# A routing search in six digits with wider steps, other spacings of its products, and one instruction pinned in order

## The chip, the cores and the metric

The kernel runs on one core of one Trainium2 chip. The metric is the device time of one execution in microseconds (us); for the kernel before it is the median of three runs. A profile is one more execution, recorded by the hardware profiler.

## The reference

Three layers follow one another: a gated linear attention, a dense layer with a leaky ReLU, and a mixture of eight experts. Only the last one's routing is touched:

```python
logits = x @ w_gate                       # 3072 tokens, 8 experts
order = np.argsort(-logits.flatten())
for idx in order:                         # best (token, expert) pair first
    tok, e = idx // E, idx % E
    if assigned[tok] >= 0 or counts[e] >= cap:   # cap = 3072 / 8 = 384
        continue
    assigned[tok] = e; counts[e] += 1
for e in range(E):                        # then each expert on its 384 tokens
    out[assigned == e] = np.maximum(x[assigned == e] @ w1[e], 0) @ w2[e]
```

The greedy pass is one long sequence: an expert that is full is closed, and its tokens go to their next choice.

## The kernel before

Attention and the first layer (`first`, `second`) take the span up to some 486 us. From there the main stream of TensorE is `layer2`: `second` for the last nine blocks of 128 tokens (products that write `xp`), the turning of the first expert's tokens (`xT`), and eight times `expert` (products that write `hp`, then `yp`). Each of these large products has 384 columns.

The routing (`route`) runs beside that stream, on VectorE with small products on TensorE. It makes seven rounds; each finds the expert that fills up first and the key of the last token that it takes, closes it, and hands a token list to `token_list` and a row of weight addresses to `fetch_weights`. In a round a 32-bit key is searched digit by digit (`LEVELS`: shift, bits, thresholds T). One level of the search is this chain: VectorE compares every token's value with T thresholds (`ge`); TensorE counts with `ge` as the weights (`c`, one product for each of NT/G = 24/(128/T) groups, of E*G columns); VectorE takes the diagonal (`cm`, `cd`); TensorE sums over partitions (`cnt`); VectorE compares with the room left (`ok`); TensorE joins the experts' bits (`tot`); VectorE finds the digit (`scr`) and takes it off the values (`v`), and the next level's `ge` follows. So T = 32 means six products of 32 columns, T = 16 three of 64 columns, and T = 64 twelve of 16 columns.

What sets the order of the instructions on each engine has two parts. A `Driver` writes the program: it adds up 160 ns for each large product (384 / 2.4) and lets a side stream go on when its pause has passed. The pauses of the routing are `GAP`: after the first comparison of a round (`GAP[4]`, 3400), after the comparison of the other levels (`GAP[0]`, 1700), after `cd` (`GAP[1]`, 700), after `ok` (`GAP[2]`, 550) and before a round's `ps` (`GAP[3]`, 2000). Then the planner of the tile framework orders each engine's instructions: of those that its own model of the times holds ready, it takes the one that the program has first. So a product whose inputs the model holds late goes further back, and a VectorE instruction that it holds ready early can move ahead of others. `keep_in_program_order` takes that freedom from one instruction: it is placed behind everything that the program already has on that engine.

At a round's end the program runs through `take`, `asg`, `un` into the next round (`m`, `eq0`, `key`, `am`, `v`, `oh`, `ge`, `dg`) with no pause until `GAP[4]`. The list of the finished round starts up to 300 ns of the driver's clock later, with `si`, `lo`, `hi`, `lob`, `hib`, and goes on with `ohs`, `h12`, `rh`, the products `pi` and `pj`, and the addresses `idx`, `row`.

`route_constants` prepares thresholds (`thr`, and scaled copies `thl`), selection and diagonal masks on VectorE just before the routing begins.

The profile gives all instructions one line, L84, since a helper records them; they are told apart by what they write.

Of the kernel before, what the change touches and what calls it, by code (L numbers as in the profile page):

```python
# [11 lines left out]
BF16 = mybir.dt.bfloat16  # L12
# [3 lines left out]
OP = mybir.AluOpType  # L16
# [75 lines left out]
def body(tc, qk, v, f_logit, w_in, w_out, w_gate, w1, w2, out):  # L92
    nc = tc.nc
    w_in, w_out = w_in.bitcast(I32), w_out.bitcast(I32)
    PE, DVE, ACT, POOL, SP = (InOrder(tc, e) for e in (nc.tensor, nc.vector, nc.scalar, nc.gpsimd, nc.sync))
# [6 lines left out]
    NT = B * S // 128  # L102
# [10 lines left out]
    with ExitStack() as ctx:  # L113
# [504 lines left out]

        LEVELS = [(27, 5, 32), (22, 5, 32), (17, 5, 32), (12, 5, 32), (7, 5, 32), (3, 4, 16), (0, 3, 16)]
        STEP = [2.0 ** (-6 * l) for l in range(len(LEVELS))]
        R = {}

        def route_constants():
            def const(name, shape, dt=F32):
                R[name] = rc.tile(shape, dt, name=name)
                return R[name]

            DVE.tensor_scalar(const("tri", [128, 128], BF16), column_less_row(rc, "jp"), 0.0, None, op0=OP.is_gt)  # L630
            DVE.memset(const("ones", [128, 128], BF16), 1.0)
            i128 = const("i128", [128, 128])
            POOL.iota(i128, pattern=[[1, 128]], base=0, channel_multiplier=0,
                      allow_small_or_imprecise_dtypes=True)
            const("place", [128, 384], F16)
            POOL.iota(const("i384", [128, 384]), pattern=[[1, 384]], base=1, channel_multiplier=0,
                      allow_small_or_imprecise_dtypes=True)
            DVE.tensor_scalar(const("i1", [128, 32]), i128[:, :32], 1.0, None, op0=OP.add)
            pi = const("pi", [128, 1], I32)
            DVE.tensor_copy(pi, pcol)  # L640
            for w in (4, 5):
                T, G = 2 ** w, 128 >> w
                thr = const(f"thr{w}", [128, NT // G, T, G], BF16)
                for a in range(NT // G):
                    DVE.tensor_copy(thr[:, a], R["i1"][:, :T, None].to_broadcast([128, T, G]))
                t = const(f"t{w}", [128, 1], I32)
                tf = const(f"tf{w}", [128, 1])
                DVE.tensor_scalar(t, pi, 7 - w, None, op0=OP.logical_shift_right)
                DVE.tensor_copy(tf, t)
                DVE.tensor_scalar(const(f"sel{w}", [128, T], F16), i128[:, :T], tf, None, op0=OP.is_equal)  # L650
                DVE.tensor_scalar(t, pi, G - 1, None, op0=OP.bitwise_and)
                DVE.tensor_copy(tf, t)
                d1 = const(f"d1{w}", [128, G])
                DVE.tensor_scalar(d1, i128[:, :G], tf, None, op0=OP.is_equal)
                DVE.tensor_copy(const(f"diag{w}", [128, E, G]), d1[:, None, :].to_broadcast([128, E, G]))
            m5 = rc.tile([128, 128], I32, name="m5")
            DVE.tensor_copy(m5, i128)
            DVE.tensor_scalar(m5, m5, 31, None, op0=OP.bitwise_and)
            m5f = rc.tile([128, 128], F32, name="m5f")
            DVE.tensor_copy(m5f, m5)  # L660
            DVE.tensor_scalar(t, pi, 2, None, op0=OP.arith_shift_right)
            sf = const("sf", [128, 1])
            DVE.tensor_copy(sf, t)
            DVE.tensor_scalar(const("join", [128, 128], F16), m5f, sf, None, op0=OP.is_equal)
            DVE.tensor_scalar(t, pi, 5, None, op0=OP.arith_shift_right)
            qf = const("qf", [128, 1])
            DVE.tensor_copy(qf, t)
            DVE.tensor_scalar(const("quarter", [128, 4]), i128[:, :4], qf, None, op0=OP.is_equal)
            DVE.tensor_copy(const("i12", [128, 12, NT], BF16), i128[:, :12, None].to_broadcast([128, 12, NT]))
            DVE.tensor_copy(const("jn", [128, 12, NT], BF16), i128[:, None, :NT].to_broadcast([128, 12, NT]))  # L670
            wd = const("wd", [128, E])
            DVE.tensor_scalar(wd, i128[:, :E], -1.0, float(E), op0=OP.mult, op1=OP.add)
            DVE.tensor_copy(const("wdt", [128, NT, E], BF16), wd[:, None, :].to_broadcast([128, NT, E]))
            DVE.tensor_copy(const("wdx", [128, E, NT], BF16), wd[:, :, None].to_broadcast([128, E, NT]))
            DVE.tensor_scalar(const("wdc", [128, 1]), pcol, -1.0, float(E), op0=OP.mult, op1=OP.add)

            pw = const("pw", [128, 1], I32)
            DVE.tensor_scalar(pw, R["wdc"], 127.0, None, op0=OP.add)
            DVE.tensor_scalar(pw, pw, 23, None, op0=OP.logical_shift_left)
            DVE.memset(const("bits", [128, 128], BF16), 0.0)  # L680
            DVE.tensor_scalar(R["bits"][:E], R["ones"][:E, :], pw.bitcast(F32)[:E], None, op0=OP.mult)
            for i in range(2):
                DVE.memset(const(f"cd{i}", [128, 128], F16), 0.0)
            DVE.tensor_scalar(const("p1024", [128, 1]), pcol, float(E * 128), None, op0=OP.add)

            n = len(LEVELS) - 1
            sh, mk = (const(x, [128, n, NT], I32) for x in ("sh", "mk"))
            unit = const("unit", [128, n, NT])
            for l, (s, w, T) in enumerate(LEVELS[1:]):
                POOL.memset(sh[:, l, :], s)  # L690
                POOL.memset(mk[:, l, :], 2 ** w - 1)
                POOL.memset(unit[:, l, :], STEP[l + 1])
            R["thr"] = [R["thr5"]]
            for l, (s, w, T) in enumerate(LEVELS):
                if l > 0:
                    t = R["thr5" if T == 32 else "thr4"]
                    u = rc.tile(list(t.shape), BF16, name=f"thl{l}")
                    DVE.tensor_scalar(u, t, STEP[l], None, op0=OP.mult)
                    R["thr"].append(u)
            DVE.tensor_scalar(const("i1s", [128, 16]), R["i1"][:, :16], STEP[-1], None, op0=OP.mult)  # L700

            DVE.tensor_copy(const("opn", [128, E]), wd)
            DVE.memset(const("un", [128, NT]), 1.0)
            DVE.memset(const("asg", [128, NT]), 0.0)
            DVE.memset(const("kcap", [128, 1]), float(NT * 128 // E))
            DVE.memset(const("smx", [128, 1]), 0.0)

        def small(shape, name, dt=F32, bufs=2):
            return rw.tile(shape, dt, name=name, bufs=bufs)

        def bank(shape, name):
            return banks[0].tile(shape, F32, name=name, tag="rt", bufs=RT)
# [3 lines left out]
        def route():  # L716
# [4 lines left out]
            wdx, kcap, un, asg, smx, ones, i1, opn = (R[x] for x in ("wdx", "kcap", "un", "asg", "smx", "ones", "i1", "opn"))  # L721
            last = [small([128, 1], f"last{i}", bufs=1) for i in range(2)]
            for rnd in range(E - 1):
# [17 lines left out]
                DVE.scalar_tensor_tensor(v, d0, 1.0, un, op0=OP.add, op1=OP.mult)  # L741
                for l, (sh, w, T) in enumerate(LEVELS):
                    G = 128 // T
                    ge = small([128, NT * 32], "ge", BF16)[:, :NT * T].rearrange("p (a t g) -> p a t g", t=T, g=G)
                    va = v.rearrange("p (a g) -> p a g", g=G)[:, :, None, :].to_broadcast([128, NT // G, T, G])
                    DVE.tensor_tensor(ge, va, R["thr"][l], op=OP.is_ge)
                    if l == 0:
# [13 lines left out]
                    with nc.allow_low_precision("one count and zeros"):  # L761
                        DVE.tensor_reduce(cd[:, :E], cm, axis=AX.X, op=OP.add)
                    yield GAP[1]
                    cnt = bank([128, 32], "cnt")
                    mm(cnt[:, :T], cd, R[f"sel{wt}"], True, True)
                    ok = small([128, 32], "ok", BF16)
                    DVE.tensor_scalar(ok[:, :T], cnt[:, :T], kcap, None, op0=OP.is_ge)
                    yield GAP[2]
                    tot = bank([128, 32], "tot")
                    mm(tot[:, :T], R["bits"], ok[:, :T], True, True)  # L770
                    J = small([128, 1], "J")
                    scr = small([128, 32], "scr")
                    DVE.tensor_scalar(scr[:, :T], tot[:, :T], STEP[l], None, op0=OP.min, op1=OP.add, accum_out=J)
                    if l + 1 < len(LEVELS):
                        vp = v
# [12 lines left out]
                                         op0=OP.is_equal, op1=OP.mult, accum_out=cg)  # L788
# [55 lines left out]
            DVE.tensor_scalar(wi, mx, -128.0, R["p1024"], op0=OP.mult, op1=OP.add)  # L844
            LISTS["w", r] = wi

        GAP = (1700.0, 700.0, 550.0, 2000.0, 3400.0)
        lists = []

        def slots_of(x, n):  # L850
# [17 lines left out]
        def token_list(r, s):  # L868

            si = small([128, NT], "si", I32)  # L870
            DVE.tensor_scalar(si, s, -1.0, None, op0=OP.add)
            lo = small([128, NT], "lo", I32)
            DVE.tensor_scalar(lo, si, 31, None, op0=OP.bitwise_and)
            hi = small([128, NT], "hi", I32)
# [7 lines left out]
            G = 4  # L882
# [447 lines left out]
```

## Time and profile before

| | |
|---|---|
| three runs | 784.7, 785.66, 787.34 us (median 785.66) |
| the profiled execution | 781.42 us, its span 779.6 us |
| TensorE's granted clock, mean | 0.983 |
| busy in the span | TensorE 730.7 us (94%), weight load 484.1, VectorE 558.8 (72%), ScalarE 350.0, GpSimd 142.7 |

The profiler observes a product's start and models its end: each large product is shown as some 0.325 us long while the next one starts 0.16 us after it. So TensorE looks busy across a gap of up to about 0.16 us, and lost time is read from the starts.

### The profile page before, as it was taken

How to read it: one execution, taken by the hardware profiler on the slowest of the kernel's cores; microseconds unless marked ns; L12 is line 12 of the kernel's file. 1: busy time of each engine (PE TensorE's matmuls, PEld its weight loads, DVE VectorE, ACT ScalarE, POOL GpSimd, SP SyncE). 2: the span in 40 equal slices, each digit the busy share in tenths (PEclk: the TensorE clock that was granted, in tenths of full speed). 3: DMA queues.
4: the chain of work that ended last, by engine and by line, in shares of the span. 5: the costliest groups of instructions: out<-in, count | busy, mean ns of one | idle time of the engine just before them, and what ended most of it. 6: DMA issues, size and time to landing. Idle time of an engine off the chain costs nothing.

```text
span 779.6 us, 15455 instructions
## 1 busy us (share of the span) xinstructions
PE 730.7 (94%) x5900; PEld 484.1 (62%) x5900; DVE 558.8 (72%) x1579; ACT 350.0 (45%) x732; POOL 142.7 (18%) x158
## 2 busy tenths in 40 slices
PE   6888998999999999998999999999989899999995
PEld 5756775677576577676666666555545455556663
DVE  5899999968966967966873958677685676873320
ACT  6566656557755754753663743000123123222320
POOL 5355312000000000000000001010243434535111
PEclk9899899999999999999999999999999999999998
DMA  9965544698897798998898500050475557665300
GB/s 258 249 162 164 161 133 125 152 276 219 237 249 213 210 309 191 250 249 221 238 272 230 166 2 2 23 192 22 148 224 155 177 158 168 228 198 174 107 31 30
DMA packets 111643, 135.90 MB, mean 174 GB/s; under 512 B 62929, under 2 KB 94674, under 8 KB 109522
## 3 DMA queue, kind: packets, MB, share of 16 engines
q1 hardware_dynamic: 106194, 100.31, 49.1%
q0 software_dynamic: 5376, 34.61, 13.1%
q8 instruction: 46, 0.75, 0.4%
q14 instruction: 27, 0.22, 0.1%
HBM read 86.52 MB, written 34.60 MB: 155 GB/s over the span
## 4 chain that ended last, share of the span: by engine, by line
PE 49%; DVE 25%; DMA 9%; issue 8%; ACT 5%; SPq 1%; POOL 1%; another core or an unknown queue 1%; POOLq 0%; ACTq 0%; DVEq 0%
PE hp L84 17%; PE xp L84 17%; PE yp L84 5%; DVE g L84 3%; PE y L84 3%; DVE winu L84 3%; DMA xw_s<-in_moe_w 3%; DMA fT<-in_f_logit 2%; DVE gl L84 2%; DVE woutu L84 2%; DMA turned<-x 2%; DVE xw_l L84 1%; PE P L84 1%; PE U L84 1%; PE c L84 1%
## 5 line engine op out<-in xcount | busy, mean ns | idle before, releaser
L84 PE MATMUL hp<-xT,winh 128*128 128x384 f16 x768 | 191.4, 329 | 11.8 <-DVE g L84 11.7
L84 PE MATMUL xp<-wo,gh 128*128 128x384 f16 x768 | 190.4, 326 | 0.8 <-DVE wo L84 0.8
L84 PE MATMUL hp<-xT,winl 128*128 128x384 f16 x384 | 126.3, 329 | 0.0
L84 PE MATMUL xp<-wo,gl 128*128 128x384 f16 x384 | 125.0, 326 | 0.0
L84 PEld LDWEIGHTS <-gh 128*128 128x128 f16 x912 | 83.9, 97 | 42.6
L84 PEld LDWEIGHTS <-winh 128*128 128x128 f16 x768 | 74.3, 99 | 57.3 <-issue 16.5
L84 PE MATMUL hp<-x2T,w1e 128*128 128x384 f16 x576 | 99.3, 325 | 0.7 <-ACT x2T L84 0.4
L84 PE MATMUL yp<-w2e,hh 128*128 128x384 f16 x384 | 94.4, 325 | 0.0
L84 ACT ACTIVATE g<-hp 128x384 f32<-128x384 f32 x152 | 73.0, 485 | 23.1 <-PE hp L84 21.5
L84 DVE SCALAR_TENSOR_TENSOR g<-hp,g 128x384 f32<-128x384 f32 x128 | 69.5, 552 | 8.2 <-ACT g L84 7.8
L84 PEld LDWEIGHTS <-w1e 128*128 128x128 f16 x576 | 52.3, 97 | 32.9 <-issue 1.1
L84 PEld LDWEIGHTS <-gl 128*128 128x128 f16 x528 | 48.7, 97 | 28.6 <-DVE gl L84 0.9
L84 ACT ACTIVATE gh<-g 128x768 f16<-128x768 f32 x64 | 53.9, 841 | 26.1 <-DVE g L84 25.4
L84 ACT ACTIVATE xw_h<-xw_s 128x768 f16<-128x768 f32 x64 | 53.2, 839 | 25.5 <-DMA xw_s<-in_moe_w 24.7
L84 POOL IOTA jp<- 128x128 f32 x2 | 0.5, 238 | 341.8 <-PE hp L84 341.7
L84 PE MATMUL yp<-w2e,hl 128*128 128x384 f16 x192 | 62.5, 325 | 0.0
L84 DVE TENSOR_TENSOR gl<-g,gh 128x768 f16<-128x768 f32 x52 | 49.7, 956 | 16.8 <-ACT gh L84 16.2
L84 DVE SCALAR_TENSOR_TENSOR xw_l<-xw_s,xw_h 128x768 f16<-128x768 f32 x64 | 60.2, 951 | 1.9 <-ACT xw_h L84 1.9
L84 ACT ACTIVATE hh<-hp 128x384 f16<-128x384 f32 x64 | 31.4, 491 | 62.2 <-PE hp L84 52.1
L84 ACT ACTIVATE x<-yp 128x384 f32<-128x384 f32 x24 | 11.8, 491 | 93.3 <-PE yp L84 75.1
L84 ACT ACTIVATE x<-xp 128x384 f16<-128x384 f32 x24 | 11.7, 489 | 92.0 <-PE xp L84 80.8
L84 PEld LDWEIGHTS <-winl 128*128 128x128 f16 x384 | 37.8, 98 | 22.9 <-issue 0.9
(265 smaller groups left out, 1228.3 us busy)
## 6 DMA issues: line engine op xcount, KB each, us to landing
xw_s<-in_moe_w SPq DMA_DIRECT2D x64, 384.0 KB, 4.0
qkT<-in_qk SPq DMA_DIRECT2D x48, 192.0 KB, 4.1
wout_s<-in_moe_w_out SPq DMA_DIRECT2D x16, 384.0 KB, 3.5
w1d<-xw_h SPq DMA_DIRECT2D x32, 192.0 KB, 4.2
w1d<-xw_l SPq DMA_DIRECT2D x32, 192.0 KB, 4.0
w2d<-xw_h SPq DMA_DIRECT2D x32, 192.0 KB, 4.3
w2d<-xw_l SPq DMA_DIRECT2D x32, 192.0 KB, 4.0
fT<-in_f_logit SPq DMA_DIRECT2D x24, 192.0 KB, 3.5
```

The source lines that it names most:

```text
L84: i = f(*args, **kwargs)
```

## The change

Six digits of 6, 6, 6, 5, 5 and 4 bits take the place of seven of 5, 5, 5, 5, 5, 4 and 3. The first three have 64 thresholds, the rest 32 (the last one too). `thr4` gives way to `thr6`, tiles are widened to 64, the thresholds are copied by one instruction for each width, two pauses are longer, and `si` is pinned.

```diff
-        LEVELS = [(27, 5, 32), (22, 5, 32), (17, 5, 32), (12, 5, 32), (7, 5, 32), (3, 4, 16), (0, 3, 16)]
-        STEP = [2.0 ** (-6 * l) for l in range(len(LEVELS))]
+        LEVELS = [(26, 6, 64), (20, 6, 64), (14, 6, 64), (9, 5, 32), (4, 5, 32), (0, 4, 32)]
+        STEP = [2.0 ** (-7 * l) for l in range(len(LEVELS))]
...
-            DVE.tensor_scalar(const("i1", [128, 32]), i128[:, :32], 1.0, None, op0=OP.add)
+            DVE.tensor_scalar(const("i1", [128, 64]), i128[:, :64], 1.0, None, op0=OP.add)
...
-            for w in (4, 5):
+            for w in (6, 5):
                 T, G = 2 ** w, 128 >> w
                 thr = const(f"thr{w}", [128, NT // G, T, G], BF16)
-                for a in range(NT // G):
-                    DVE.tensor_copy(thr[:, a], R["i1"][:, :T, None].to_broadcast([128, T, G]))
+                DVE.tensor_copy(thr, R["i1"][:, None, :T, None].to_broadcast([128, NT // G, T, G]))
...
-            R["thr"] = [R["thr5"]]
+            R["thr"] = [R["thr6"]]
...
-                    t = R["thr5" if T == 32 else "thr4"]
+                    t = R["thr5" if T == 32 else "thr6"]
...
-            DVE.tensor_scalar(const("i1s", [128, 16]), R["i1"][:, :16], STEP[-1], None, op0=OP.mult)
+            DVE.tensor_scalar(const("i1s", [128, 32]), R["i1"][:, :32], STEP[-1], None, op0=OP.mult)
...
-                    ge = small([128, NT * 32], "ge", BF16)[:, :NT * T].rearrange("p (a t g) -> p a t g", t=T, g=G)
+                    ge = small([128, NT * 64], "ge", BF16)[:, :NT * T].rearrange("p (a t g) -> p a t g", t=T, g=G)
...
-        GAP = (1700.0, 700.0, 550.0, 2000.0, 3400.0)
+        GAP = (2000.0, 700.0, 550.0, 2000.0, 4000.0)
...
-            DVE.tensor_scalar(si, s, -1.0, None, op0=OP.add)
+            tc.keep_in_program_order(DVE.tensor_scalar(si, s, -1.0, None, op0=OP.add))
```

`cnt`, `ok`, `tot` and `scr` are widened from 32 to 64 in the same way.

## Rows read from the trace of the kernel before

**Rows 1.** Windows: stretch, then each engine's busy us (instructions), clock, DMA share, GB/s.
```profile
486.00:705.00 219.00, 207.04 (x1589) 120.72 (x1588) 156.99 (x808) 43.03 (x93) 67.93 (x70) 1.00 0.49 153
```

**Rows 2.** TensorE's groups by form, 486 to 705: count, busy us, mean ns, idle before.
```profile
L84 PE MATMUL hp<-x2T,w1e 128*128 128x384 f16 x402 | 70.3, 325 | 0.3 <-issue 0.3
L84 PE MATMUL xp<-wo,gh 128*128 128x384 f16 x258 | 64.6, 325 | 0.0
L84 PE MATMUL yp<-w2e,hh 128*128 128x384 f16 x240 | 59.3, 325 | 0.0
L84 PE MATMUL xp<-wo,gl 128*128 128x384 f16 x130 | 42.2, 325 | 0.0
L84 PE MATMUL yp<-w2e,hl 128*128 128x384 f16 x120 | 39.0, 325 | 0.0
L84 PE MATMUL c<-oh,ge 128*128 128x32 bf16 x210 | 10.9, 178 | 5.9 <-DVE ge L84 5.6
...
L84 PE MATMUL c<-oh,ge 128*128 128x64 bf16 x42 | 3.5, 193 | 0.0
```

**Rows 3.** TensorE's waits, 486 to 705: total us, times, longest.
```profile
PE c L84 <- DVE ge L84: 5.6, 6, 2.2
PE cnt L84 <- DVE cd L84: 2.5, 2, 2.2
```

**Rows 4.** Timeline, one level of the first round: start us, us, instruction [idle before].
```profile
493.34 0.18 PE L84 MATMUL tot<-ok,bits 128*128 128x32 bf16 x1
...
494.08 0.56 DVE L84 TENSOR_TENSOR ge<-v,thl 128x768 bf16<-128x768 bf16 x1
...
494.34 0.33 PE L84 MATMUL xp<-wo,gl 128*128 128x384 f16 x1
494.69 0.22 PEld L84 LDWEIGHTS <-ge 128*128 128x128 bf16 x6 [0.42 <-DVE ge L84]
494.70 0.32 PE L84 MATMUL c<-oh,ge 128*128 128x32 bf16 x6
```

**Rows 5.** Timeline of TensorE, one level of the second round.
```profile
532.93 0.17 PE L84 MATMUL tot<-ok,bits 128*128 128x16 bf16 x1
532.96 0.49 PE L84 MATMUL xp<-wo,gh 128*128 128x384 f16 x2
...
534.58 0.25 PE L84 MATMUL c<-oh,ge 128*128 128x64 bf16 x3
```

**Rows 6.** VectorE's groups by form, 486 to 705.
```profile
L84 DVE TENSOR_TENSOR ge<-v,thl 128x768 bf16<-128x768 bf16 x28 | 15.6, 556 | 0.7
L84 DVE SCALAR_TENSOR_TENSOR hl<-hp,hh 128x384 f16<-128x384 f32 x22 | 12.2, 553 | 0.9 <-ACT hh L84 0.7
...
L84 DVE TENSOR_TENSOR ge<-v,thl 128x384 bf16<-128x384 bf16 x14 | 5.0, 357 | 0.4
```

**Rows 7.** Timelines of VectorE and TensorE at the starts of two rounds.
```profile
541.79 0.17 DVE L84 TENSOR_SCALAR si<-sl 128x24 int32<-128x24 f32 x1
541.87 0.30 DVE L84 TENSOR_TENSOR di<-di,mk 128x144 int32<-128x144 int32 x1
...
543.00 0.56 DVE L84 TENSOR_TENSOR ge<-v,thr 128x768 bf16<-128x768 bf16 x1
...
542.89 0.33 PE L84 MATMUL xp<-wo,gh 128*128 128x384 f16 x1
543.62 0.32 PE L84 MATMUL c<-oh,ge 128*128 128x32 bf16 x6 [0.40 <-DVE ge L84]
...
669.26 0.17 DVE L84 TENSOR_SCALAR si<-sl 128x24 int32<-128x24 f32 x1
```

**Rows 8.** Timeline of VectorE, two disturbed places.
```profile
570.72 1.43 DVE L84 TENSOR_TENSOR inc<-inc,totc 128x48 f32<-128x48 f32 x1
...
621.46 0.19 DVE L84 TENSOR_TENSOR cm<-c,diag 128x32 f16<-128x32 f32 x1 [3.36 <-remote]
```

**Rows 9.** Timeline of VectorE, the last of the constants.
```profile
484.27 1.48 DVE L84 TENSOR_SCALAR thl<-thr 128x768 bf16<-128x768 bf16 x6
```

More of the change, by code (lines that the diff above doesn't have):

```diff
@@ L763, in route @@
                     yield GAP[1]
-                    cnt = bank([128, 32], "cnt")
+                    cnt = bank([128, 64], "cnt")
                     mm(cnt[:, :T], cd, R[f"sel{wt}"], True, True)
-                    ok = small([128, 32], "ok", BF16)
+                    ok = small([128, 64], "ok", BF16)
                     DVE.tensor_scalar(ok[:, :T], cnt[:, :T], kcap, None, op0=OP.is_ge)
                     yield GAP[2]
-                    tot = bank([128, 32], "tot")
+                    tot = bank([128, 64], "tot")
                     mm(tot[:, :T], R["bits"], ok[:, :T], True, True)
                     J = small([128, 1], "J")
-                    scr = small([128, 32], "scr")
+                    scr = small([128, 64], "scr")
                     DVE.tensor_scalar(scr[:, :T], tot[:, :T], STEP[l], None, op0=OP.min, op1=OP.add, accum_out=J)
```

## The prediction

> **What bounds the kernel now.** I read the page's busy shares first, then the windows, the groups by form, the waits, and last the timelines of single levels of the search. The busy shares say TensorE, at 94%. The routing runs from 486 to 705 us, and in that stretch TensorE is busy for 207.0 of 219.0 us at the full clock (granted 1.00, the 2.4 GHz level), VectorE for 157.0 [rows 1]. So the routing matters only by what it takes from TensorE: its own products, and the time in which TensorE stands before one of them.
>
> The second part is larger than the busy column shows. Ten large products start between 532.96 and 534.58, one in 0.162 us, though each is drawn 0.325 long [rows 5, 2]. The stretch holds 402 + 258 + 240 + 130 + 120 = 1150 of them [rows 2], which is 186.3 us. A `c` product of 32 columns costs 0.025: six weight loads span 0.22 from the first start to the last end, and 0.22 less one load's own 0.096 over five steps is 0.025 [rows 4]. One of 64 columns costs 0.028: three span 0.25, and less one's own 0.193 over two steps that is 0.028 [rows 5, 2]. So the 252 `c` products cost 210 x 0.025 + 42 x 0.028 = 6.4 us [rows 2], and the other 190 or so small ones, at 0.025 to 0.06, some 7. Together about 200 of 219 us: TensorE loses some 19. Of that, 8.1 us are shown as waits of the search: 5.6 for `ge` (six times), 2.5 for `cd` [rows 3]. The rest hides under the drawn ends.
>
> How it hides is seen in one level of the first round: `tot` starts at 493.34, seven large products follow, the last at 494.34, and `c` starts not at 494.50 but at 494.70, because `ge`, begun at 494.08, has just ended [rows 4]. TensorE loses 0.2 us, and the way from `tot` to the next `c` takes 1.36 us. In the second round, at 532.93, ten products stand between `tot` and `c`, and nothing is lost [rows 5]. The difference is the planner: where its model holds the routing late against the program, it puts each product as early as it thinks `ge` is done, and it is optimistic by 0.2 us; where the routing is in step, the program's pause (1700 / 160 = 10.6 products) decides. By the starts, 14 of the 49 levels lose 0.13 to 0.2 us in this way, some 2.4 us in all.
>
> Five rounds begin with a longer loss. At 543.62 the first `c` is 0.56 late (the large one before it, at 542.89, would have made room at 543.05), after `ge` that began at 543.00 [rows 7]; the other four lose 2.2 (the longest wait for `ge`, [rows 3]), 1.0, 0.5 and 0.6, together about 5.
>
> **The change part by part.**
>
> *Products.* A round has 5 x 6 + 2 x 3 = 36 `c` products now and 3 x 12 + 3 x 6 = 54 after. Now: 30 x 0.025 + 6 x 0.028 = 0.92 us. After, if twelve columns fewer cost nothing less, 54 x 0.025 = 1.35. Seven rounds: +3.0 us. One `cnt` and one `tot` go from each round, 14 at about 0.025: -0.35. Sum +2.6. A product of 16 columns is not in the trace. Its ends: half of the 32-column row, 0.0125 (after: 0.45 + 0.45 = 0.90 a round, so -0.1 and with the 14 others -0.5), and the 64-column row, 0.028 (after: 36 x 0.028 + 0.45 = 1.46, so +3.8, and +3.4). I take 0.025, since 64 columns cost only 0.003 more than 32: what is paid here is the product, hardly its columns. The Trainium skill ("TensorE: Matmul & The Clock Gate", "Wait — 56ns, not 53.3ns?") says that successive starts are never closer than about 25 ns, however few the columns. By that rule the term is +2.6, by columns alone -0.5; the trace at 32 columns agrees with it, and no row has 16.
>
> *A level less.* The chain of a level is shorter by one in each round, but TensorE has other products to run, so only the losses count. In the first round all levels are tight; one goes, -0.2. In later rounds the pauses sum to 4.0 + 5 x 2.0 + 6 x 1.25 + 2.0 = 23.5 us where they were 3.4 + 6 x 1.7 + 7 x 1.25 + 2.0 = 24.35, and the longer single pauses put a round in step sooner: I take two or three fewer tight levels, -0.4. Together -0.6; bounds: -2.4 (all tight levels gone) and +2.6 (13 of them losing 0.2 more, because `ge` is longer than the planner holds).
>
> *The comparison.* From 384 to 768 elements `ge` goes from 357 to 556 ns [rows 6], 0.2 us for 384. So 1536 elements come to 0.556 + 0.40 = 0.96 us. From `tot` to `c` that makes 1.36 + 0.40 = 1.77 us in the wide levels. The new pause gives 2000 / 160 = 12.5 products, 2.0 us: room of 0.25, where it was 10.6 x 0.162 - 1.36 = 0.36. An `hl` of 0.55 us [rows 6] in between breaks it. In step this costs nothing, as now. VectorE's comparisons in a round: 3 x 0.96 + 3 x 0.556 = 4.55 us for 5 x 0.556 + 2 x 0.357 = 3.49, and the other instructions of one level go: at worst +1.06 x 7 = 7.4 us, and VectorE has 219 - 157 = 62 us free in the stretch [rows 1].
>
> *The pinned `si`.* In the second round's end `si` starts at 541.79 and the next instruction at 541.87 [rows 7], 0.09 a piece; `lo` and `hi` depend on it and stand before `ge` too. Placed behind the next round's `dg`, they no longer delay the first comparison: -0.27 in each of five rounds, if the product's place stays. I take -0.2 x 5 = -1.0. Bounds: -1.35, and +2.0 (the first comparison's own +0.40 five times, `GAP[4]` notwithstanding: 4000 / 160 = 25 products, while the trace has 26 to 34 between `ps` and `c`, so the planner, not the pause, sets that place). What speaks for the upper end: in the last round `si` comes at 669.26, behind `ge` already [rows 7], and its first `c` loses 0.6 all the same. Queued behind the pinned instruction on VectorE is the list alone, and the lists' products `pi` come some 40 large products after `ps`; the gathers wait much longer than the 0.5 us that a list is later.
>
> *Constants.* Six `thl` take 1.48 us [rows 9], 0.25 each; then two of double length and three: about 1.9. The seven fewer copies give some of it back. The routing begins up to 0.5 us later, beside the 432 products of `second` that TensorE has then: nothing. Without that cover, +0.5.
>
> *The sum.* 2.6 - 0.6 - 1.0 + 0 = +1.0 us. The profiled execution took 781.42 us (span 779.6), so 782.4. The runs' median, 785.66, is 4.24 above the profiled execution; carried over, 786.7.
>
> *What no term holds.* Two places in the rows are disturbed from outside the search: `inc`, a sum over 48 columns, takes 1.43 us, and VectorE stands for 3.36 us before `cm` for something that the profile calls remote [rows 8]. They lie behind the longest waits, 2.2 for `ge` and 2.2 for `cd` [rows 3]. After the change these moments shift, so the 4 us can go or come more often: I count 0, and 3 us to either side in the range.
>
> **The rivals.**
>
> *The spacing removes the waits (faster).* If 12.5 and 25 products' room lets every product come in step, the tight levels' 2.4 us go, and of the rounds' first waits the 0.55 that each of five has without a disturbance, 2.75; of the `cd` waits 0.9. With the products' +2.6: -3.4, so 782.2. For it: in step nothing is lost [rows 5]. Against it: the first `c` stands 26 to 34 products after `ps` already, beyond the new pause, so the planner still comes late into most rounds.
>
> *The wide comparison comes after its product (slower).* One mechanism: the planner sets the wide levels' `c` as tight as it does in rows 4, and its model is short not by 0.2 but by up to the whole 0.40 that the comparison grows; also in step, an `hl` of 0.55 exceeds the room of 0.25. It decides where `c` is fewer than eleven large products (1.77 / 0.162) behind `tot`. There are 21 wide comparisons; if ten lose 0.40 more, +4.0 on the sum: 790.7. For it: all first rounds' levels and 14 in total are tight. Against it: two lengths of `ge`, 357 and 556 ns, lead to about the same loss, so the model seems to know how length grows.
>
> *The pin does nothing.* If the first waits stay at 0.55, as the last round suggests, the third term is 0: 787.7, still within a few tenths of a per cent.
>
> **How the numbers follow.** What can be told from no change is 0.3% of 785.66, 2.4 us: below 783.3 is faster, above 788.0 slower. Forecast (786.7, own spread 784 to 789) 0.32; the pin does nothing (787.7) 0.13; spacing removes the waits (782.2) 0.29; comparison late (790.7) 0.26. The first two fall within the bound with 0.39 of their 0.45, and above it with 0.05; the third is faster, the fourth slower with a little within. So faster 0.30, same 0.41, slower 0.29. The range reaches to both outer cases and 1 us beyond for the disturbances: 780.8 to 791.5.
>
> **What would show it.** Right: 378 `c` products with starts 0.025 apart, wide comparisons of 0.95 to 0.97 us, `si` behind `ge` and `dg` in every round, first `c` of a round 0.3 to 0.4 late, fewer tight levels, and 84 instead of 98 `cnt` and `tot`. Wrong: `c` products of 16 columns nearer 0.0125 or above 0.03; wide comparisons of 1.6 us; TensorE's waits for `ge` falling under 3 us or rising over 9; or a large difference outside 476 to 710 us, where the change has no instruction.

## The result: slower by 1.4%, and the profile after

The changed kernel takes 795.96 us (median of six runs, 794.73 to 797.23) beside 785.19 of the kernel before (six runs, 784.09 to 787.34): ratio 1.0141, interval 1.0102 to 1.0181. Forecast was 786.7. Its profiled execution took 794.78 us, 13.4 more than that of before.

The stretch of the routing, which answers to [rows 1]; columns as there:
```profile
486.00:705.00 219.00, 200.97 (x1622) 116.62 (x1621) 158.00 (x742) 39.28 (x85) 63.80 (x64) 0.99 0.46 143
```
TensorE's groups by form from 486 to 720 us, beside [rows 2]:
```profile
L84 PE MATMUL c<-oh,ge 128*128 128x16 bf16 x252 | 9.7, 176 | 7.3 <-DVE ge L84 7.2
L84 PE MATMUL c<-oh,ge 128*128 128x32 bf16 x126 | 6.5, 177 | 2.0 <-DVE ge L84 1.2 <-issue 0.5
```
TensorE's waits there (total us, times, longest), beside [rows 3]:
```profile
PE c L84 <- DVE ge L84: 8.4, 6, 2.3
PE tot L84 <- DVE ok L84: 2.2, 2, 1.6
PE ps L84 <- DVE x L84: 2.0, 4, 0.7
```
VectorE's comparisons by form, beside [rows 6]:
```profile
L84 DVE TENSOR_TENSOR ge<-v,thl 128x1536 bf16<-128x1536 bf16 x14 | 13.4, 959 | 0.4
L84 DVE TENSOR_TENSOR ge<-v,thl 128x768 bf16<-128x768 bf16 x21 | 11.7, 557 | 0.7
```
TensorE has more to do and is busy for 6 us less of the same 219: it stands more. VectorE is as busy as before. The products and comparisons are of the forecast number and size; the waits are not.

To see all lost time I went by starts, from 480 to 715 us: the start of a product, less that of the one before it, less that one's own step (0.025 for a small product, 0.057 for `xT`, 0.162 for a large one). So TensorE loses 19.3 us before the change and 29.7 after: before `c` 9.1 and 13.4, before `cnt` and `tot` 4.3 and 6.6, before `ps` 1.0 and 3.0. With the products' 2.6 that is 13.0. Of the 13.4, 1.7 lie ahead of the routing's first `c`, which starts at 490.99 instead of 489.28 (the last section shows why); so 11.7 were to be found, and the count is good to about 1 us.

Some 1.5 us of it are no waits. Behind two losses close together (1.41 us before `cnt`, 0.83 before `tot`) the granted clock falls (columns as in [rows 1]):
```profile
650.00:652.00 2.00, 0.69 (x4) 0.34 (x5) 0.35 (x2) 0.00 (x0) 0.99 (x1) 1.00 0.77 188
652.00:654.00 2.00, 1.57 (x6) 0.76 (x6) 1.32 (x5) 0.00 (x0) 0.00 (x0) 0.52 1.11 229
654.00:656.00 2.00, 2.00 (x13) 1.06 (x12) 0.00 (x0) 0.00 (x0) 0.00 (x0) 0.63 0.51 99
```
TensorE was busy for 0.69 of 2.00 us; then the clock is mostly at its lower level of 1.2 GHz, and large products start 0.32 us apart instead of 0.16. The first profile of before has no such stretch in the routing.

Where a long loss comes from is seen at the end of a round. A timeline of all engines after the change (start us, us, instruction [idle before]):
```profile
633.16 0.95 POOL L84 TENSOR_TENSOR hl<-g,hh 128x384 f16<-128x384 f32 x1 [2.21 <-ACT g L84]
633.25 0.89 DVE L84 TENSOR_SCALAR es<-wd,mx 128x8 f32<-128x8 f32 x1
...
636.21 1.00 POOL L84 TENSOR_TENSOR hl<-g,hh 128x384 f16<-128x384 f32 x1 [2.10 <-DVE s L84]
636.36 0.92 DVE L84 TENSOR_TENSOR s<-s,x 128x48 f32<-128x48 f32 x1
...
638.90 0.55 DVE L84 SCALAR_TENSOR_TENSOR hl<-hp,hh 128x384 f16<-128x384 f32 x1
...
639.93 0.95 DVE L84 TENSOR_TENSOR ge<-v,thr 128x1536 bf16<-128x1536 bf16 x1
640.79 0.17 DVE L84 TENSOR_SCALAR si<-sl 128x24 int32<-128x24 f32 x1
...
640.93 0.47 PE L84 MATMUL c<-oh,ge 128*128 128x16 bf16 x12 [1.65 <-DVE ge L84]
```
The same `es` in all seven rounds (minimum, median and maximum in ns):
```profile
L84 DVE TENSOR_SCALAR es<-wd,mx x7: 219/227/228, 508.6 to 693.0; 128x8 f32<-128x8 f32 x7
```
```profile
L84 DVE TENSOR_SCALAR es<-wd,mx x7: 220/224/890, 509.6 to 699.6; 128x8 f32<-128x8 f32 x7
```
The first line is of before, the second of after. An instruction of 0.22 us takes 0.89 because it began while GpSimd's `hl` ran, and it ends 0.03 after it; `s` goes from 0.20 to 0.92 in the same way. VectorE works them off one after the other, and the first comparison stands behind them, so the 1.4 us arrive at `c`, which is 1.81 late by the starts. I call this a collision: an instruction over 0.3 us longer than its form's median, that ends just after GpSimd's `hl`. Before has 7 (the `inc` of [rows 8] is one), after has 12. The Trainium skill ("SBUF — State Buffer", "SBUF: two separate sides") says that GpSimd and some VectorE instructions, those with two inputs in SBUF among them, take one pair of ports whole, and the later one waits for all of the other. `s`, with two inputs, agrees: it ends 0.07 us after an `hl` of 1.00. Two places don't fit: `inc` before (1.43 us) and `un` after (1.60 us) begin 0.43 and 0.64 us ahead of the drawn start of their `hl`, so by that rule they should not have waited for it.

A second kind is that of `cm` in [rows 8]: TensorE's signal comes late. Places where VectorE, waiting for `c`, `cnt` or `tot`, starts over 0.6 us after the drawn end of the product: two before (4.2 us together), six after (7.4).

### The profile page after: what moved, and what is told of

Its sections match the earlier page's. It is cut to its first block, busy times and chain, and to the rows that moved or that the text cites. A ratio compares the mean times of both kernels' runs of the same rounds, so it can differ in the third digit from the quotient of the medians.

```text
span 793.0 us, 15620 instructions
## 1 busy us (share of the span) xinstructions
PE 738.9 (93%) x6012; PEld 488.7 (62%) x6012; DVE 564.0 (71%) x1522; ACT 349.5 (44%) x732; POOL 142.7 (18%) x155
## 4 chain that ended last, share of the span: by engine, by line
PE 57%; DVE 24%; issue 8%; DMA 6%; ACT 4%; POOL 1%; SPq 0%; POOLq 0%; DVEq 0%; ACTq 0%
PE hp L84 19%; PE xp L84 18%; PE yp L84 7%; PE y L84 3%; DVE winu L84 3%; DMA fT<-in_f_logit 2%; PE P L84 2%; DVE g L84 2%; PE A L84 2%; PE c L84 2%; DVE woutu L84 1%; PE U L84 1%; DMA turned<-x 1%; DMA xw_s<-in_moe_w 1%; DVE qs L84 1%
## 5 line engine op out<-in xcount | busy, mean ns | idle before, releaser
L84 PE MATMUL yp<-w2e,hh 128*128 128x384 f16 x384 | 96.3, 329 | 0.0
L84 ACT ACTIVATE x<-xp 128x384 f16<-128x384 f32 x24 | 11.7, 488 | 92.0 <-PE xp L84 83.9
```

The costliest lines, as they stand in the source:

```text
L84: i = f(*args, **kwargs)
```

## The experiments

The first edits are made of these four hunks: digits (the digits, thresholds and tiles of the change), pauses, pin, and `hl` (with the fourth, the 24 copies `g` that ScalarE makes for GpSimd go too):
```diff
+        LEVELS = [(26, 6, 64), (20, 6, 64), (14, 6, 64), (9, 5, 32), (4, 5, 32), (0, 4, 32)]
+        GAP = (2000.0, 700.0, 550.0, 2000.0, 4000.0)
+            tc.keep_in_program_order(DVE.tensor_scalar(si, s, -1.0, None, op0=OP.add))
-                    if f % 2 == 0 and r < E - 2:
+                    if False:
```
The theory after the first profile: collisions make the loss; rivals: the longer comparisons, the pauses, or the pin make it. A table of all results stands at the end.

**Parts alone.** Digits alone (first hunk), pauses alone (second), pin alone (third), each on the kernel before, and the changed kernel with every `hl` on VectorE (fourth).

> Six digits (6, 6, 6, 5, 5, 4 bits) with the old pauses and no pinned instruction. Wide-comparison theory (the loss is the longer chain from tot to c): this kernel carries most of the loss of the full change, +8 to +14 us over before, with more waits of c for ge. Phase theory (the rounds' ends fall beside GpSimd's hl because of all three edits together): +2.6 us for the products and anything between -2 and +8 for the waits, with VectorE's stretched instructions showing which. Pause theory (the longer pauses cost): near +2.6 us.

> Seven digits as before, only the two pauses longer (2000 for 1700, 4000 for 3400). Pause theory: rounds are 2.4 us longer in the driver's clock (six times 0.3 and 0.6), so their ends drift into the experts' hp phase and this kernel alone loses +5 us or more. Wide-comparison theory: 0 or a gain of up to 3 us, since the products come later than their comparisons.

> Seven digits, old pauses, only si pinned. My forecast had -1.0 us for it (first comparison of a round 0.2 us earlier in five rounds). If the pin does nothing: within 1 us of before. If it makes the lists' products late: waits of pi grow, +2 us or more.

> The changed kernel with every hl of the experts on VectorE (one instruction of 0.55 us) instead of every second one on GpSimd with an extra copy on ScalarE. GpSimd theory (16 VectorE instructions are stretched by some 0.7 us each while GpSimd's hl runs, 9.5 us in the changed kernel and 6.4 in the one before): the stretched instructions go and the waits of c at the starts of rounds shrink by 0.7 to 1.5 us each, so -4 us or more against the changed kernel. Wide-comparison theory: VectorE has 24 times 0.55 us more to do, so no gain or up to 4 us lost.

Measured: 1.0120, 1.0336, 0.9981 and 1.0051. Digits alone bring most of the loss, within the 8 to 14 us that the rival of the longer comparisons gave them; the pin alone does nothing that can be told. What speaks against the longer comparisons is the fourth run. Without `hl` on GpSimd there is no collision left, and the waits of [rows 3] shrink in the changed kernel to
```profile
PE c L84 <- DVE ge L84: 1.3, 5, 0.4
PE pi L84 <- DVE rh L84: 1.1, 2, 0.8
PE ps L84 <- DVE x L84: 0.4, 1, 0.4
```
Seven digits with the longer pauses are another case: there the lists come too late, and TensorE waits once for the tokens (and then runs at the lower clock, another 5.0 us in its profile):
```profile
PE hp L84 <- DMA x2T<-xg: 12.4, 1, 12.4
```

**`hl` in the kernel before, and the pin taken out.** The kernel before with the fourth hunk; with the third and fourth; the changed kernel without the third; and a collision put back, on the kernel before with the fourth:
```diff
+                pz = small([128, 384], "pz")
+                POOL.tensor_tensor(pz, R["i384"], mx.to_broadcast([128, 384]), op=OP.mult)
```

> The kernel before with every hl of the experts on VectorE. GpSimd theory: the seven stretched instructions go (6.4 us there), so 2 to 6 us faster than before, and the changed kernel treated the same way stays 1.5 to 4 us above this one: the products (+2.6 us) and the longer comparisons, which are what the change costs by itself. Wide-comparison theory: the changed kernel treated the same way stays 7 us or more above this one.

> The changed kernel without the pinned si: six digits and the longer pauses. If the pin moves list instructions off the first comparison's way but costs nothing else, this is 0 to 2 us slower than the full change, so 1.014 to 1.018 of before; if the pin is what hurts in the full change, this stands near 1.012 or below.

> The kernel before with every hl on VectorE, and one GpSimd instruction of 384 elements added at the end of each round (a product of a constant with the closed expert's number, which nobody reads). GpSimd theory: a VectorE instruction of the round's end stretches by up to 0.7 us beside each of the seven, and the first c of a round comes that much later: +2 to +5 us against the same kernel without them. If GpSimd's work beside VectorE is harmless: within 1 us of it.

> Seven digits, old pauses, si pinned, every hl on VectorE: the version that the first runs point to. Pinned alone gave 0.998 of before; with GpSimd off the routing's way 0.990 to 0.996 of before, the fastest of all so far.

Measured: 1.0030, 1.0105, 1.0134 and 1.0013. The first was expected 2 to 6 us faster and the fourth at 0.990 to 0.996, so both missed: the seven collisions are gone, but 24 more `hl` run on VectorE and the late signals are 5.7 and 5.4 us. With every `hl` moved in both kernels the change costs 1.0051 / 1.0030 = 1.002, 1.6 us. So most of the loss depends on where `hl` runs. It is no clean price of the change, though: the two ran on different chips, and only the seven digits have late signals there. The kernel without the pin, at 1.0105, came out where the pin was said to hurt; the intervals overlap, so that stays open. The added instruction cost 8 us where 2 to 5 were expected, and not cleanly: its waits are
```profile
PE ps L84 <- DVE x L84: 5.4, 7, 1.9
PE cnt L84 <- DVE cd L84: 5.1, 3, 2.7
```
where without it they were
```profile
PE cnt L84 <- DVE cd L84: 4.4, 3, 2.1
...
PE ps L84 <- DVE x L84: 0.6, 1, 0.6
```
`ps` now waits in all seven rounds, and only three instructions are stretched. The order has changed too, so this run shows a price of GpSimd's work at a round's end, not of the collision alone.

**Both kernels again on one chip, the late signals, and a tuned version.** In the third run plain copies replace the DMA transposes, so the turning of five experts' tokens is left out; the fourth has the changed kernel with the fourth hunk and other pauses.
```diff
-                SP.dma_start(xt[:, :, 128 * m:128 * (m + 1)], xg[m], transpose=True)
+                SP.dma_start(xt[:, :, 128 * m:128 * (m + 1)], xg[m].rearrange("p (a b) -> p a b", b=128))
```
```diff
-                    yield GAP[0] if l else GAP[4]
+                    yield (GAP[0] if T == 64 else 1700.0) if l else GAP[4]
...
+        GAP = (2000.0, 700.0, 550.0, 2000.0, 5000.0)
```

> The kernel before, unchanged, for its profile on the same chip as the next runs. Ratio 1.000. By the theory of collisions (each `hl` of GpSimd, 0.9 to 1.0 us, can stretch one small VectorE instruction by about 0.7 us, and those at the rounds' ends delay a `c`), its stretched instructions stay near 7 and its losses before small products, by the starts from 480 us, near 20 us. If places of collision are drawn anew in each execution, the count may be anything from 5 to 12.

> The changed kernel, unchanged, on the same chip. Ratio 1.012 to 1.018. By the theory of collisions: the same places as in its first profile (some 12 stretched VectorE instructions, losses before small products near 30 us), since the places are set by the order of the instructions. If the extra loss were chance of one profile, the places would differ and the losses would be nearer 20.

> The changed kernel with the five DMA transposes of each later list's tokens turned into plain copies of the same bytes: the turning of the tokens of five experts is left out, nothing else. If the DMA transposes hold back VectorE's starts (places of 1.2 to 2.5 us before `cm`, `ok`, `scr`), those places go: losses fall by some 4 to 6 us, ratio 1.007 to 1.010. If they don't, the places stay and the ratio stays at 1.012 to 1.018.

> Six digits and the pinned instruction, every `hl` on VectorE, the long pause after a comparison (2000) only for the 64 thresholds and 1700 for the others, 5000 in place of 4000 after a round's first comparison. If what is left of the late first comparisons (6 to 7 us before `c`) is a pause too short, they fall under 4 us and the ratio is 0.998 to 1.003. If the planner and not the pause sets the place of these products, nothing changes against the same kernel with 4000 and 2000: 1.005.

Measured: 1.0038, 1.0178, 1.0175, 1.0083. The places of collision are set by the order of the instructions: again 7 and 12, and of the 12 the same ones. The round end shown above, in this second profile:
```profile
637.48 0.95 POOL L84 TENSOR_TENSOR hl<-g,hh 128x384 f16<-128x384 f32 x1 [2.21 <-ACT g L84]
637.58 0.89 DVE L84 TENSOR_SCALAR es<-wd,mx 128x8 f32<-128x8 f32 x1
...
640.54 1.00 POOL L84 TENSOR_TENSOR hl<-g,hh 128x384 f16<-128x384 f32 x1 [2.10 <-DVE s L84]
640.68 0.92 DVE L84 TENSOR_TENSOR s<-s,x 128x48 f32<-128x48 f32 x1
...
645.26 0.39 PE L84 MATMUL c<-oh,ge 128*128 128x16 bf16 x9 [1.65 <-DVE ge L84]
```
The late signals don't come from turning by DMA: with plain copies six places stay, 6.2 us. The tuned version has no collision, but eight late signals, 9.4 us together; its pauses didn't shorten the losses before `c` (6.7), and it is slower than both of its expectations. And the kernel before against itself gives 1.0038: intervals here are too narrow by about 0.4%, so the 1.0030 of the kernel before with `hl` moved can't be told from 1.

**Only the rounds' ends.** `hl` goes to VectorE only between a round's last digit and the next round's first `c`: in the changed kernel, in the kernel before, and there with the pin. Beside them digits alone with the fourth hunk.
```diff
                     yield GAP[0] if l else GAP[4]
+                    TAIL[0] = False
...
                     yield GAP[2]
+                    TAIL[0] = l + 1 == len(LEVELS)
...
-                    if f % 2 == 0 and r < E - 2:
+                    if f % 2 == 0 and r < E - 2 and not TAIL[0]:
```

> The changed kernel with GpSimd's `hl` moved to VectorE only while the routing is between a round's last digit and the next round's first `c`; the others stay on GpSimd. If the collisions at the rounds' ends make the loss: stretched instructions of the ends go, the first `c` of rounds comes at most 0.6 us late as before, losses before `c` fall from 13.5 to some 8 us, ratio 1.006 to 1.010. If collisions inside a round count as much, ratio 1.012 or more.

> The kernel before with the same move. It has some seven collisions of 0.4 to 1.2 us, most at rounds' ends, two first `c` late by 1 us or more. By the theory these go: ratio 0.994 to 0.999. If `hl` on VectorE costs as much there as the collisions did: 1.000 to 1.004, as with every `hl` moved.

> Seven digits, `si` pinned, and the same move: the version that the runs point to, 0.998 for the pin alone and the collisions of the rounds' ends away. By the theory 0.992 to 0.998; if the move brings nothing, 0.998 to 1.003.

> Six digits alone, old pauses, nothing pinned, every `hl` on VectorE. If six digits cost only their products (2.6 us), the ratio is that of the kernel before with `hl` moved plus 0.3%: 1.004 to 1.008. If what six digits lost on their own (1.012) were not collisions but the longer comparisons, it stays at 1.010 to 1.015.

Measured: 1.0135, 0.9933, 0.9943, 1.0039. In the changed kernel my theory failed as a whole explanation: five collisions are left, the losses before `c` fall from 13.4 to 8.2 as expected, and the time hardly moves, since the late signals grew to 10.9 us. The largest of them, in the timeline:
```profile
616.78 0.46 PE L84 MATMUL c<-oh,ge 128*128 128x16 bf16 x12
616.92 4.41 SPq L84 DMA_TRANSPOSE x2T<-xg  x3
...
617.85 0.99 POOL L84 DMA_INDIRECT out<-x,idx  x1 [0.30 <-issue]
619.92 0.17 DVE L84 TENSOR_TENSOR cm<-c,diag 128x16 f16<-128x16 f32 x1 [3.20 <-remote]
...
620.36 0.20 PE L84 MATMUL cnt<-sel,cd 128*128 128x64 f16 x1 [2.46 <-DVE cd L84]
```
`c` is drawn as ended at 617.24; VectorE, idle, gets its signal 2.68 us later, and TensorE stands for 2.46 before `cnt`.

**The version that beats both, once more**, beside the kernel before against itself.

> The kernel before with GpSimd's `hl` moved to VectorE only at the rounds' ends, a second time and longer. If the collisions there cost what their losses before `c` suggest (some 3 us): 0.994 to 0.998. If the 0.993 of the first time was scatter: 0.998 to 1.003, like the kernel before against itself.

> The kernel before against itself, a second time: 0.997 to 1.003. It shows how wide the scatter of one comparison is.

Measured: 0.9969 and 1.0007. With both times, the kernel before with only the rounds' ends' `hl` moved is some 0.5% faster than before, 779.5 to 780 us; by the scatter of 0.4% this is likely, not certain.

All kernels, by digits. Collisions, the sum of late signals and losses are of one profile each; the losses hold what the lower clock takes, 1.1 to 2.6 us in twelve of the profiles and 5.0 in that of the pauses alone:

| kernel | ratio, interval | collisions | late signals, us | losses, us |
|---|---|---|---|---|
| six: changed | 1.0141 (1.0102 to 1.0181) | 12 | 7.4 | 29.7 |
| changed, again | 1.0178 (1.0115 to 1.0240) | 12 | 6.2 | 27.6 |
| plain copies | 1.0175 (1.0120 to 1.0230) | 12 | 6.2 | 28.9 |
| `hl` moved at ends | 1.0135 (1.0099 to 1.0170) | 5 | 10.9 | 27.5 |
| digits alone | 1.0120 (1.0054 to 1.0187) | 9 | 0 | 21.9 |
| without pin | 1.0105 (1.0064 to 1.0146) | 11 | 4.7 | 26.0 |
| tuned | 1.0083 (1.0049 to 1.0116) | 0 | 9.4 | 26.4 |
| every `hl` moved | 1.0051 (1.0018 to 1.0084) | 0 | 0 | 15.1 |
| digits alone, `hl` moved | 1.0039 (1.0006 to 1.0072) | 0 | 0 | 19.9 |
| seven: pauses alone | 1.0336 (1.0271 to 1.0400) | 11 | 0 | 30.8 |
| `hl` moved, `pz` added | 1.0134 (1.0091 to 1.0177) | 3 | 5.5 | 27.4 |
| before, again | 1.0038 (1.0001 to 1.0075) | 7 | 4.8 | 23.4 |
| before, third time | 1.0007 (0.9974 to 1.0040) | 7 | 3.8 | 20.5 |
| `hl` moved | 1.0030 (1.0004 to 1.0056) | 0 | 5.7 | 22.0 |
| pin, `hl` moved | 1.0013 (0.9986 to 1.0040) | 0 | 5.4 | 20.1 |
| pin alone | 0.9981 (0.9950 to 1.0012) | 7 | 0 | 15.7 |
| pin, `hl` moved at ends | 0.9943 (0.9915 to 0.9971) | 1 | 4.0 | 16.2 |
| `hl` moved at ends | 0.9933 (0.9899 to 0.9967) | 2 | 1.4 | 19.2 |
| the same, again | 0.9969 (0.9939 to 0.9999) | 2 | 3.4 | 18.6 |

Among six digits, the two kernels with neither disturbance are 0.4 to 0.5% slower than before, those with one or both 0.8 to 1.8%. The kernel before has both itself. No seven digits without either were measured; beside the fastest, with 2 collisions and 1.4 or 3.4 us of late signals, these two are 0.7 to 1.2% slower.

## Why the prediction was wrong

- *Products, +2.6: right.* 378 `c` products; 190 of 231 successive starts are exactly 25 ns apart, at 16 columns as at 32. `cnt` and `tot` are 84. The Trainium skill's floor of about 25 ns ("TensorE: Matmul & The Clock Gate", "Wait — 56ns, not 53.3ns?") holds for 16 columns too.
- *Comparison: right.* 0.96 us was forecast, 0.959 and 0.949 measured; in the round whose end has no collision the first `c` loses 0.55, as before. So the rival of the late comparison is not what happened, though the time went to its side and beyond.
- *A level less, -0.6: wrong.* By the starts, and without the rounds' first, 18 levels lose 0.12 to 0.23 us, 3.0 together; before 13 lost 2.3. Measured +0.7.
- *Constants, 0: right.* From the start of the first layer's `hp` products to the first `c`: 445.8 us before, 445.0 after.
- *The pin, -1.0: wrong.* `si` stands behind `dg` at all six rounds' ends, but behind `ge` only at three. At the others it comes ahead of `oh` and `ge`, which the program has before it, so the pin does not hold it behind everything, as the description of the kernel has it:
```profile
576.73 0.17 DVE L84 TENSOR_SCALAR si<-sl 128x24 int32<-128x24 f32 x1
...
577.08 0.95 DVE L84 TENSOR_TENSOR ge<-v,thr 128x1536 bf16<-128x1536 bf16 x1
...
578.41 0.16 DVE L84 TENSOR_SCALAR lo<-si 128x24 int32<-128x24 int32 x1
```
  `lo` and `hi` do leave the way of the first comparison at all six, and it gains nothing: where no collision comes in, the first `c` loses 0.55 us as before. The first products of five rounds lose 0.55, 2.5, 2.0, 1.8 and 1.1 us where they lost 0.56, 2.3, 1.0, 0.5 and 0.6: +3.0, from the collisions. The pin alone measured 0.998.
- *"What no term holds", 0 with 3 to either side: the step that failed.* I took `inc` and `cm` of [rows 8] for two odd places that shift, and the range in the end held only about 1 us beyond the outer rivals for them. They were the visible part of two classes. Collisions go from 7 to 12 and enter the first products' +3.0 and the losses before `ps` (+2.0); late signals go from two to six, and `cnt` and `tot` lose 2.3 us more. The lower clock (1.5) and the later start (1.7) come on top. In the next execution the collisions came at the same instructions and six signals were late again, so these two are a property of the program; the lower clock did not come back in it. The rows held this: an `inc` of 1.43 us for a normal 0.20 should have sent me to what else ran then, and to a count.

Shown: GpSimd's `hl` stretches VectorE's instructions, and with `hl` off GpSimd the changed kernel falls from 1.014 to 1.005 of before. Not shown: what the change costs by itself, since every kernel with seven digits has collisions or late signals or both: 0.2% beside seven digits with `hl` moved, some 1% beside the fastest seven digits. Open: why TensorE's signals come late, and why this order meets more of them. With the first `c` of the ends mended, they took the place of what was won; whether by chance of this order was not tried.

## What to carry to other kernels

Where two engines hold each other up, a chain of small dependent instructions is priced by what runs beside it, not by its own length: count stretched instructions (a form's maximum beside its median) before moving anything. A change that only shifts the phase of a side stream can cost more than its own instructions. Take the shared work away from the part where every instruction waits for the last, and leave it elsewhere; here that likely won 0.5% in the kernel before, and nothing in the changed one.

## What the runs showed of the hardware

An execution's start varies for every kernel alike. Windows of the first layer, of before and after from 30 us and of after again from 40 us, in this order (columns as in [rows 1]):
```profile
30.00:40.00 10.00, 9.43 (x80) 8.72 (x81) 7.28 (x14) 5.72 (x17) 1.10 (x2) 0.84 0.88 165
```
```profile
30.00:40.00 10.00, 10.00 (x54) 9.45 (x54) 5.72 (x11) 3.18 (x11) 0.89 (x1) 0.50 1.02 229
```
```profile
40.00:50.00 10.00, 10.00 (x58) 9.14 (x58) 5.74 (x11) 5.67 (x16) 1.19 (x1) 0.50 0.34 80
```
TensorE's granted clock stays at 0.50, the 1.2 GHz level, until some 40 or 50 us in some executions, though TensorE was busy for 7.5 us of 20 to 30 in all three, and the first layer's `hp` products begin at 43.5, 46.0 or 50.8 us. It is no effect of the change: of three profiles of before, two begin at 43.5 and 43.7, one at 46.4, and one of seven digits with the pin at 50.7. But on one chip it made 5.8 of the 11.2 us between the two profiles. The clock falls in the routing too: 13 of the 20 profiles have one or two stretches at the lower level there, each behind a stand of TensorE. Not every stand brings one: in the first profile of before TensorE is busy for 0.08 us of 620 to 622, and the clock stays at 1.00.

The other surprise is a signal of TensorE that comes up to 3.1 us late (with the pin and every `hl` moved). Where `cm` is held in [rows 8], ScalarE is held too, and both go on within 0.04 us; the timeline of before has
```profile
621.50 0.49 ACT L84 ACTIVATE hh<-hp 128x384 f16<-128x384 f32 x1 [3.34 <-remote]
```
So it is TensorE's signal that is late, not VectorE. All 61 late signals of the 20 profiles lie 0.5 to 5.0 us behind the start of one of GpSimd's gathers of a list's tokens (`xg`); elsewhere VectorE starts some 0.04 us behind the drawn end. The gathers are not shown to be the cause: no run moves them, and five profiles have them and no late signal.
